# Sliding-window attention and a gated feed-forward layer: batch 0 prepared unit by unit on TensorE

## The chip, the cores and the metric

The kernel runs on one core of a Trainium2 chip. The metric is the device time of one execution in microseconds (us), given as the median of several runs. The core has a matrix engine (TensorE, PE in the profile; its weight loads have a row of their own, PEld), a vector engine (VectorE, DVE), a scalar engine (ScalarE, ACT), GpSimd (POOL) and SyncE (SP). DMA transfers are issued from a queue on SP, ACT or POOL; here POOL issues all loads that change the type from float32 to float16, and SP the output and the first loads. Matmuls read SBUF and write PSUM; DVE and ACT read both.

## What is computed

```python
# q, k, v: 8 batches x 8 heads x 576 positions x 64, float32
scores = scale * q @ k.T                        # scale = 1/8
mask = (rel >= 0) & (rel < 64)                  # rel = query position - key position
attn = softmax(where(mask, scores, -1e9))
x = (attn @ v), heads side by side              # 4608 tokens x 512
out = (relu(x @ w_gate) * (x @ w_val)) @ w_out  # 512 -> 1536 -> 512
```

## The kernel before

The 4608 tokens are cut into 24 units of 192 (three a batch, all eight heads). Two units make a tile of 384 tokens, so there are 12 tiles. A query block of 64 needs its own 64 keys and the 64 before it; a unit is three such windows.

**The attention of a unit.** `qk_load` brings k and q of a whole batch with positions on partitions; `qk_trans` (L181) turns them with 32x32 block transposes on DVE (four of 128x576 a batch). `u_st` (L236) makes the scores, keys on partitions, in 48 matmuls of 32 rows. `u_exp` takes the exponentials on ACT, `u_mask` multiplies with the band mask on DVE. `u_pv_wide` (L302) multiplies with v, of which each head has 64 columns of ones beside its values, so that values and row sums come out together. `u_copy` copies the values out of PSUM on ACT, `u_sum` (L331) turns the sums on DVE, `u_back` takes the reciprocals and turns them back, and `u_norm` (L352) writes the normalized values to `xt`, the input of the feed-forward layer. Units 0 and 1 go another way: their mask is added to the scores as a matmul with a bias (`u_bias`, L201), and their sums come from matmuls with `ones`.

**v.** A window needs 128 rows of v. `v_load` (L188) loads each block of 64 into the upper partitions of a window, and `v_low` (L194) copies it on DVE to the lower partitions of the next one. There are three buffers, one for each unit of a batch; `v_ones` sets the columns of ones.

**The feed-forward layer.** `hidden` (L389) makes, for each of 12 blocks of 128 columns, the gate and the value product (4 matmuls each of 384 or, for one unit, 192 columns), ACT applies relu, DVE multiplies the two (L407). `output` (L447) and `output_by_rows` (L474) make the product with w_out. PSUM is split between two pools: `f_ps` with four buffers of one bank (scores of unit 0, hidden and output products) and `a_ps` with two buffers of two banks (attention).

**The order.** Each engine executes its instructions in the order of the program. The order is made by `Weaver` (L16): functions are put in with a planned time, the matmuls of the feed-forward layer advance a planned clock, and whatever is due is emitted ahead of the next matmuls. `w_load` notes a planned landing time for each third of a weight matrix (L513 to L522), and `w_need` advances the clock to it. The kernel begins with a few matmuls on zeros (`heat`, L213), the loads of batch 0, and units 0 and 1; from L578 on the feed-forward layer sets the order, and units are woven in.

Of the kernel before, what the change touches and what calls it, by code (L numbers as in the profile page):

```python
# [9 lines left out]
FP32 = mybir.dt.float32  # L10
FP16 = mybir.dt.float16
ACT = mybir.ActivationFunctionType
MUL = mybir.AluOpType.mult

# [28 lines left out]
def kernel(  # L43
# [43 lines left out]
    v16s = [persist.tile([128, UB, H, 128], FP16, name=f"v16_{i}") for i in range(UB)]  # L87
# [4 lines left out]
    ident = consts.tile([128, 128], FP16)  # L92

# [21 lines left out]
    def v_ones(i, eng):  # L115
        eng.memset(v16s[i][64 if i == 0 else 0:, 0, :, 64:128], 1.0)
        for w in range(1, UB):
            eng.memset(v16s[i][:, w, :, 64:128], 1.0)  # L118

    def k_zeros():  # L120
        nc.vector.memset(kTs[1][:, :, 0:64], 0.0)

    def constants():
        nc.vector.memset(kTs[0][:, :, 0:64], 0.0)
        nc.vector.memset(v16s[0][0:64, 0], 0.0)
        nc.vector.memset(ones, 1.0)
        nc.vector.memset(ones0, 1.0)
        nc.vector.memset(ones0[0:64], 0.0)

# [40 lines left out]
    def k_first(hh):  # L170

        k32 = nat["k32", hh] = x_sb.tile([128, S // 32 * D], FP32, name="k32", bufs=2)
        nc.sync.dma_start(k32, k[0, G * hh:G * hh + G].rearrange("h (i j) d -> (h i) (j d)", i=32))

    def k_round(hh, part, parts):
        n = S // 32 * D // parts
        if part == 0:
            nat[0, "k", hh] = a_in.tile([128, S // 32 * D], FP16, name=f"k{hh}", bufs=2)
        nc.scalar.copy(nat[0, "k", hh][:, n * part:n * part + n], nat["k32", hh][:, n * part:n * part + n])  # L179
# [8 lines left out]
    def v_load(u):  # L188
        b, uu = divmod(u, UB)
        for w in range(UB):  # L190
            k0 = U * uu + 64 * w
            nc.gpsimd.dma_start(v16s[uu][64:128, w, :, 0:64], v[b, :, k0:k0 + 64].rearrange("h p d -> p h d"))  # L192

    def v_low(u):  # L194

        uu = u % UB
        if uu > 0:
            nc.vector.tensor_copy(v16s[uu][0:64, 0, :, 0:64], v16s[uu - 1][64:128, UB - 1, :, 0:64])
        nc.vector.tensor_copy(v16s[uu][0:64, 1:UB, :, 0:64], v16s[uu][64:128, 0:UB - 1, :, 0:64])

    def u_bias(u, gs=range(G)):  # L201
# [4 lines left out]
        d["biased"] = True  # L206
# [29 lines left out]
    def u_st(u, hhs=(0, 1)):  # L236
# [3 lines left out]
        if not biased:  # L240
            st_tiles(u)
# [30 lines left out]
    def u_pv(u, cs=(0, 2, 1, 3)):  # L272
        if u > 1:
            return u_pv_wide(u)
# [351 lines left out]
```

The softmax here doesn't subtract the row's maximum and nothing guards it: scores larger than these inputs give would overflow.

## Time and profile before

| | |
|---|---|
| median of 5 runs | 339.07 us (338.83 to 340.18) |
| the profiled execution: its time | 339.07 us |
| the profiled execution: its span | 337.2 us |
| PE busy | 323.4 us, 96% of the span |
| DVE busy | 260.2 us, 77% |
| ACT busy | 176.5 us, 52% |
| POOL busy | 74.0 us, 22% |
| first feed-forward matmul | 17.17 us |

The profile is that of one execution. The span runs from the first to the last instruction; the time of the execution is 1.87 us longer. A row of busy tenths has 40 slices of equal length, of 8.4 us here. In a list of groups, the numbers behind the count are the busy time in us and the mean of one in ns, then the idle time of the engine just ahead of the group and what ended it. In a timeline, a line gives start and length in us, engine, source line and operation; "[0.83 <-DVE xt L356]" means that the engine stood idle for 0.83 us and that the write of xt on line 356 ended it. The chain of waits follows the work back from the last instruction, at each step to what released it. Busy time of PE is modelled: a PE that is always busy need not be at its peak.

### The profile page before, as it was taken

How to read it: one execution, taken by the hardware profiler on the slowest of the kernel's cores; microseconds unless marked ns; L12 is line 12 of the kernel's file. 1: busy time of each engine (PE TensorE's matmuls, PEld its weight loads, DVE VectorE, ACT ScalarE, POOL GpSimd, SP SyncE). 2: the span in 40 equal slices, each digit the busy share in tenths (PEclk: the TensorE clock that was granted, in tenths of full speed). 3: DMA queues.
4: the chain of work that ended last, by engine and by line, in shares of the span. 5: the costliest groups of instructions: out<-in, count | busy, mean ns of one | idle time of the engine just before them, and what ended most of it. 6: DMA issues, size and time to landing. Idle time of an engine off the chain costs nothing.

```text
span 337.2 us, 8605 instructions
## 1 busy us (share of the span) xinstructions
PE 323.4 (96%) x3522; PEld 195.8 (58%) x3522; DVE 260.2 (77%) x493; ACT 176.5 (52%) x383; POOL 74.0 (22%) x121
## 2 busy tenths in 40 slices
PE   7689998999999999999999999999999999999995
PEld 3475485856546656655655655654655664664653
DVE  5878969988998875897888984888889874884430
ACT  4546165745637546645555565564564664653321
POOL 8724342240213221320210410150120200000000
PEclk9999999999999999999999999999999999999999
DMA  8999997395343932491242953295214502001002
GB/s 215 178 207 198 203 212 130 25 150 87 26 78 49 156 66 56 32 187 64 18 54 72 116 82 87 18 150 116 18 10 111 32 3 93 2 2 73 22 0 95
DMA packets 52887, 29.45 MB, mean 87 GB/s; under 512 B 39280, under 2 KB 44272, under 8 KB 52848
## 3 DMA queue, kind: packets, MB, share of 16 engines
q0 software_dynamic: 47088, 18.29, 47.3%
q1 hardware_dynamic: 5616, 10.55, 8.7%
q8 instruction: 27, 0.44, 0.5%
q14 instruction: 12, 0.10, 0.1%
q10 hardware_dynamic: 144, 0.07, 0.1%
HBM read 37.75 MB, written 9.44 MB: 140 GB/s over the span
## 4 chain that ended last, share of the span: by engine, by line
PE 79%; DVE 12%; DMA 5%; issue 2%; ACT 1%; DVEq 0%; ACTq 0%; POOLq 0%
PE h L419 49%; PE op L433 22%; DMA q<-in_q_dram 5%; PE pv L311 4%; PE st L249 3%; DVE qT L186 2%; DVE sT L341 2%; DVE xt L356 2%; DVE kT L186 1%; DVE g_sb L407 1%; DVE rs L350 1%; DVE p L270 1%; PE op L465 1%; ACT xv L325 1%; DVE v L118 1%
## 5 line engine op out<-in xcount | busy, mean ns | idle before, releaser
L419 PE MATMUL h<-xt,wg 128*128 128x384 f16 (+1 forms) x640 | 116.2, 310 | 2.7 <-DVE xt L356 2.7
L419 PE MATMUL h<-xt,wv 128*128 128x384 f16 (+1 forms) x640 | 116.3, 310 | 1.0 <-DVE g_sb L407 1.0
L407 DVE TENSOR_TENSOR g_sb<-r_sb,h 128x384 f16<-128x384 f32 x144 | 78.1, 549 | 48.3 <-PE h L419 46.6
L404 ACT ACTIVATE r_sb<-h 128x384 f32<-128x384 f32 x144 | 70.1, 492 | 66.6 <-PE h L419 54.8
L433 PE MATMUL op<-wo,g_sb 128*128 128x512 f16 x420 | 93.0, 379 | 0.0
L192 POOL DMA_DIRECT2D v<-in_v_dram x72 | 49.5, 697 | 180.3 <-PE pv L311 94.9
L419 PEld LDWEIGHTS <-wg 128*128 128x128 f16 x640 | 60.5, 98 | 37.6 <-DVE xt L356 2.6
L419 PEld LDWEIGHTS <-wv 128*128 128x128 f16 x640 | 58.7, 98 | 31.7 <-issue 1.3
L433 PEld LDWEIGHTS <-g_sb 128*128 128x128 f16 x420 | 40.3, 98 | 46.5
L341 DVE STREAM_TRANSPOSE sT<-pv 64x384 f32<-64x384 f32 x88 | 51.1, 580 | 9.7 <-PE pv L311 7.7
L329 ACT COPY xv<-pv 64x384 f32<-64x384 f32 x88 | 41.5, 472 | 21.3 <-DVE sT L341 8.2
L440 ACT COPY o_sb<-op 128x512 f32<-128x512 f32 x35 | 20.5, 586 | 54.6 <-PE op L433 54.6
L263 ACT ACTIVATE p<-st 128x384 f16<-128x384 f32 x92 | 39.7, 491 | 4.2 <-PE st L249 4.1
L270 DVE TENSOR_TENSOR p<-p,mask 128x384 f16<-128x384 f16 x88 | 27.5, 352 | 0.3 <-ACT p L263 0.2
L350 DVE STREAM_TRANSPOSE rs<-rT 128x768 f32<-128x768 f32 x24 | 23.5, 978 | 0.8
L356 DVE TENSOR_TENSOR xt<-xv,rs 128x768 f16<-128x768 f32 x24 | 22.7, 948 | 0.8
L311 PEld LDWEIGHTS <-v 128*128 128x128 f16 x528 | 18.6, 98 | 3.9 <-issue 0.8
L186 DVE STREAM_TRANSPOSE kT<-k 128x576 f32<-128x576 f32 (+1 forms) x18 | 19.7, 1121 | 1.3 <-ACT k L179 1.2
L311 PE MATMUL pv<-p,v 128*128 128x64 f16 x528 | 19.7, 193 | 0.8 <-DVE p L270 0.6
L186 DVE STREAM_TRANSPOSE qT<-q 128x576 f32<-128x576 f32 x16 | 19.0, 1238 | 1.1 <-DMA q<-in_q_dram 1.1
L249 PEld LDWEIGHTS <-kT 32*128 32x128 f16 x1152 | 11.0, 92 | 10.5 <-issue 10.4
L249 PE MATMUL st<-qT,kT 32*128 32x64 f16 x1152 | 13.9, 189 | 2.8 <-DVE qT L186 2.5
(47 smaller groups left out, 90.6 us busy)
## 6 DMA issues: line engine op xcount, KB each, us to landing
out_dram<-o_sb SPq DMA_DIRECT2D x35, 256.0 KB, 2.0
q<-in_q_dram POOLq DMA_DIRECT2D x16, 288.0 KB, 7.6
v<-in_v_dram POOLq DMA_DIRECT2D x72, 64.0 KB, 3.1
k<-in_k_dram POOLq DMA_DIRECT2D x14, 288.0 KB, 5.8
wg<-in_moe_w_gate_dram POOLq DMA_DIRECT2D x3, 512.0 KB, 10.0
wv<-in_moe_w_val_dram POOLq DMA_DIRECT2D x3, 512.0 KB, 12.1
wo<-in_moe_w_out_dram POOLq DMA_DIRECT2D x3, 512.0 KB, 13.8
k<-in_k_dram SPq DMA_DIRECT2D x2, 576.0 KB, 3.9
```

The costliest lines, as they stand in the source:

```text
L186: nc.vector.transpose(dst.rearrange("p (i j) -> p j i", i=32)[:, j0:j1], src[:, j0:j1])
L192: nc.gpsimd.dma_start(v16s[uu][64:128, w, :, 0:64], v[b, :, k0:k0 + 64].rearrange("h p d -> p h d"))
L249: nc.tensor.matmul(d["st"][hh][g][:, c:c + 64], kT[rows, hh, ks + 64 * w:ks + 64 * w + 128, dh], qT[rows, hh, ks + 64 * w:ks + 64 * w + 64 ...
L263: nc.scalar.activation(d["p"][g].rearrange("p h c -> p (h c)"), d["st"][0][g][:, 0:2 * U], ACT.Exp, scale=scale)
L270: nc.vector.tensor_tensor(p, p, mask[:, None, :].to_broadcast([128, 2 * UB, 64]), MUL)
L311: nc.tensor.matmul(d["pv"][c % 2][:, c // 2, e, 64 * w:64 * w + 64], v16[:, w, 128 * h - 64 * e:128 * h - 64 * e + 128], d["p"][h % G][:, ...
L329: nc.scalar.copy(d["xs"][rows, n::2], d["pv"][n][rows, :, e, 0:U])
L341: nc.vector.transpose(to[64 * e:64 * e + 64, half::2], d["pv"][half][64 - 64 * e:128 - 64 * e, :, e, 0:U])
L404: nc.scalar.activation(part(r_sb), part(h1), ACT.Relu)
L407: nc.vector.tensor_tensor(g_sb[:, f:f + w, c0:c1], part(r_sb), part(h2), MUL)
L419: nc.tensor.matmul(h[:, b * n:b * n + n], wt[:, c, (f + b) * 128:(f + b) * 128 + 128], xt[:, c, c0:c1], start=(c == 0), stop=(c == NC - 1))
L433: nc.tensor.matmul(op, g_sb[:, f, bass.ds(sub * 128, 128)], wo[:, f], start=(f == 0), stop=(f == NF - 1))
```

## The change

Units 0 to 2, the whole of batch 0, are prepared one by one. k and q of such a unit, all heads, come in one transfer each, positions on partitions (`all_load`; unit 0's in float32 by SP, rounded half on DVE and half on ACT). TensorE turns them with matmuls against a permuted identity (`turn`), 24 each, and `unit_keep` copies the result from PSUM into `kA` and `qA` with 64 rows a head. The scores are 24 matmuls of 64 rows; all three units get their mask as a bias. The row sums are made first, by matmuls with ones (`n_sums`); `n_turn` turns them, takes the reciprocals and turns back, two heads' pairs at a time; the values follow (`n_vals`), and `n_norm` multiplies them out of PSUM straight into `xt`, without a copy.

v has one buffer for a whole batch, two in all, with nine windows. Four odd windows are loaded with 128 partitions and the last half window by itself (five transfers a batch in place of nine), and `v_spread` copies their halves to the even windows, on GpSimd, for units 4 and 5 on ACT. The fixed parts of v and k (ones, zeros) are set on GpSimd.

Units 3 to 5 get k and q by units too (`unit_loads`, four transfers; `unit_trans`, four block transposes of 128x192). From batch 2 on k and q are handled as before; their early transposes are planned 1.2 us ahead of where they were. The output of tile 0 is moved behind the first half of tile 1's hidden part, and the planned times are new.

```diff
-    v16s = [persist.tile([128, UB, H, 128], FP16, name=f"v16_{i}") for i in range(UB)]
+    kA = persist.tile([128, G, 64 + S], FP16)
+    qA = persist.tile([128, G, S], FP16)
+    NG = S // 64
+    v16s = [persist.tile([128, NG, H, 128], FP16, name=f"v16_{i}") for i in range(2)]
...
+    def v_fixed(i, eng, parts=((0, NG),)):
+        for g0, g1 in parts:
+            eng.memset(v16s[i][:, g0:g1, :, 64:128].bitcast(FP32), ONE_ONE)
+        eng.memset(v16s[i][0:64, 0].bitcast(FP32), 0.0)
...
+        nc.vector.tensor_copy(turn, ident.rearrange("p (i h) -> p h i", h=H))
...
+    def unit_flip(name, u):
+        flipped[name, u] = a_ps.tile([128, 2, 512], FP32, name=f"{name}f", tag="a")
+        to = flipped[name, u].rearrange("p a b -> p (a b)")
+        for j in range(JA):
+            for hh in range(2):
+                nc.tensor.matmul(to[64 * hh:64 * hh + 64, 64 * j:64 * j + 64],
+                                 nat[name, u][:, D * j:D * j + D],
+                                 turn[:, G * hh:G * hh + G],
+                                 start=True, stop=True, skip_group_check=True)
+
+    def unit_keep(name, u, cc, copy):
+        c0 = U * u + (64 if name == "k" else 0)
+        gs_ = slice(2 * cc, 2 * cc + 2)
+        src = flipped[name, u].rearrange("p a b -> p (a b)")[:, 0:64 * JA].rearrange("p (j g i) -> p g i j", j=JA, g=G)
+        dst = (qA if name == "q" else kA)[:, gs_, c0:c0 + U].rearrange("p g (i j) -> p g i j", j=JA)
+        copy(dst, src[:, gs_])
...
+    def v_spread(u, copy=None):
+        b, uu = divmod(u, UB)
+        t = v16s[b % 2]
+        copy = copy or nc.vector.tensor_copy
+        for g0, g1 in (((0, 3),), ((4, 5),), ((6, 7),))[uu]:
+            copy(t[64:128, g0:g1:2, :, 0:64], t[0:64, g0 + 1:g1 + 1:2, :, 0:64])
+        for g0, g1 in (((2, 3),), ((4, 5),), ((6, 9),))[uu]:
+            copy(t[0:64, g0:g1:2, :, 0:64], t[64:128, g0 - 1:g1 - 1:2, :, 0:64])
...
         if u == 0:
-            d["st"] = [[one("st") for _ in range(G)]]
-            halves = [two("st") for _ in range(2)]
...
+            d["st"] = [None] * G
+            for c in (0, 2, 1, 3):
+                d["st"][c] = f_ps.tile([128, 512], FP32, name="st", tag="h")
+            d["spare"] = d["st"][3][:, 384:512]
...
+            halves = [a_ps.tile([128, 2, 512], FP32, name="st", tag="a") for _ in range(2)]
+            d["st"] = [halves[g % 2][:, g // 2] if u < UB else halves[g // 2][:, g % 2] for g in range(G)]
...
+    def n_turn(u, r):
+        d = units[u]
+        nb = 2 * U // 32
+        sN = a_n.tile([128, nb, 32], FP32, name="sN")
+        nc.vector.transpose(sN.rearrange("p b c -> p (b c)"), d["sums"][r])
+        rN = a_n.tile([128, nb, 1], FP32, name="rN")
+        nc.vector.reciprocal(rN, sN[:, :, 0:1])
+        d["rs", r] = a_n.tile([128, nb, 32], FP32, name="rsN")
+        nc.vector.transpose(d["rs", r], rN.to_broadcast([128, nb, 32]))
+
+    def n_norm(u, r):
+        d = units[u]
+        c0 = U * (u % 2)
+        nc.vector.tensor_tensor(xt_tile(u // 2)[:, r::2, c0:c0 + U],
+                                d["pv"][r].rearrange("p (s c) -> p s c", s=2),
+                                d["rs", r].rearrange("p (s b) c -> p s (b c)", s=2), MUL)
...
-        W.at(T + (3.3 if u == 2 else 1.4 if u < 6 else -2.0), lambda: v_low(u))
+        if u > 5:
+            W.at(T - 3.0, lambda: v_spread(u, nc.gpsimd.tensor_copy))
...
-        heat(12, units[0]["st"][1][3])
+        heat(9, units[0]["st"][3])
         bands()
+        for name in "kq":
+            all_load(name, 1)
+        v_load(0, ((1, 0, 128), (3, 0, 64)))
+        v_load(1, ((3, 64, 128), (5, 0, 128)))
+        for wt, t in ((G3[0], 14.4), (V3[0], 17.0), (G3[1], 19.6)):
+            w_load(*wt, t)
+        all_load("k", 2)
         constants()
...
+        all_round("k", 0, (dve, act))
+        all_round("q", 0, (dve, act))
+        unit_flip("k", 0)
+        u_bias(0)
+        unit_flip("q", 0)
+        for name in "kq":
+            unit_keep(name, 0, 0, dve)
+            unit_keep(name, 0, 1, act)
+        heat(4, units[0]["spare"], False)
+        u_st(0)
+        for c in order:
+            u_exp(0, c)
+        for name in "kq":
+            unit_flip(name, 1)
+            for cc in range(2):
+                unit_keep(name, 1, cc, act)
+        v_spread(0, pool)
+        v_spread(1, pool)
+        all_load("q", 2)
+        v_load(2)
+        for wt, t in ((V3[1], 25.6), (G3[2], 28.2), (V3[2], 30.8)):
+            w_load(*wt, t)
+        v_fixed(1, nc.gpsimd)
+        unit_loads(3)
+        v_spread(2, pool)
+        v_load(3)
+        for n in range(3):
+            w_load(*O3[n], 38.2 + 2.6 * n)
...
+        for r in range(2):
+            n_sums(0, r)
+            n_turn(0, r)
+        heat(3, flipped["k", 1][:, 1, 256:512])
+        for r in range(2):
+            n_vals(0, r)
+            n_norm(0, r)
+        u_bias(1)
+        u_st(1)
+        for c in order:
+            u_exp(1, c)
+        for r in range(2):
+            n_sums(1, r)
+            n_turn(1, r)
...
+        finish_unit(1, 15.75, 0.01)
+        W.at(23.4, lambda: [unit_flip(name, 2) for name in "kq"] and None)
+        W.at(23.5, lambda: [unit_keep(name, 2, cc, act) for name in "kq" for cc in range(2)] and None)
+        W.at(24.2, lambda: u_bias(2))
+        W.at(24.8, lambda: u_st(2))
...
+        for u, t in ((3, 39.5), (4, 49.5), (5, 57.5)):
+            plan_trans(u, t - 3.2)
+            if u > 3:
+                W.at(t + 0.5, lambda u=u: v_spread(u, act))
+            plan_unit(u, t)
-        T = 67.0
-        early, late = (-7.4, -6.0, -4.6, -3.2), (-20.3, -18.9, -17.5, -16.1)
+        T = 69.3
+        early, late = (-8.6, -7.2, -5.8, -4.4), (-20.3, -18.9, -17.5, -16.1)
...
-        output_by_rows(0)
         ready(3)
         hidden(1, 0, U)
+        output_by_rows(0)
         output(1, (0,))
```

## The prediction

> **What bounds the kernel now.** I read the page's busy shares and slices first, the chain of waits second, then the timelines of TensorE (PE) and GpSimd (POOL), and the groups by shape for prices.
>
> ```profile
> PE 323.4 (96%) x3522; PEld 195.8 (58%) x3522; DVE 260.2 (77%) x493; ACT 176.5 (52%) x383; POOL 74.0 (22%) x121
> PE   7689998999999999999999999999999999999995
> DMA  8999997395343932491242953295214502001002
> ```
>
> PE is full from the third slice on, so the end moves only with the start of the feed-forward matmuls, with PE work added or removed after it, and with the gaps that remain. The transfers are nearly full for seven slices of 8.4 us, to about 59 us.
>
> ```profile
> 1.31 6.02 DMA q<-in_q_dram
> 7.36 1.26 DVE qT L186
> ...
> 16.16 0.96 DVE xt L356
> ...
> 119.37 7.77 PE op L433 x36
> ...
> 171.98 7.77 PE op L433 x36
> ...
> 197.93 7.77 PE op L433 x36
> ```
>
> The chain (start, length) runs through the load of q, the block transposes on VectorE (DVE), unit 0's softmax and the write of xt before PE may start. Later it is PE alone: from one tile's output to the next it is 197.93-171.98 = 25.95 us, but 52.61 us for the two tiles 119.37 to 171.98. So 0.71 us is lost there; the same occurs from 197.93 to 250.54.
>
> ```profile
> 17.17 1.48 PE L419 MATMUL h<-xt,wg 128*128 128x192 f16 x16 [0.83 <-DVE xt L356]
> 35.62 7.93 PE L433 MATMUL op<-wo,g_sb 128*128 128x512 f16 x36
> 74.10 0.81 PE L419 MATMUL h<-xt,wg 128*128 128x384 f16 x4
> ```
>
> These three marks are my yardstick: the first feed-forward matmul at 17.17, the hidden part of tile 0 done at 35.62, tile 2 begun at 74.10.
>
> ```profile
> 17.89 0.76 POOL L151 DMA_DIRECT2D wo<-in_moe_w_out_dram  x1 [2.35 <-DMA wv<-in_moe_w_val_dram]
> 23.17 0.74 POOL L151 DMA_DIRECT2D wo<-in_moe_w_out_dram  x1 [2.02 <-DMA wv<-in_moe_w_val_dram]
> L407 DVE TENSOR_TENSOR g_sb<-r_sb,h 128x384 f16<-128x384 f32 x144 | 78.1, 549 | 48.3 <-PE h L419 46.6 <-ACT r_sb L404 0.3
> L341 DVE STREAM_TRANSPOSE sT<-pv 64x384 f32<-64x384 f32 x88 | 51.1, 580 | 9.7 <-PE pv L311 7.7
> L350 DVE STREAM_TRANSPOSE rs<-rT 128x768 f32<-128x768 f32 x24 | 23.5, 978 | 0.8
> L199 DVE COPY v<-v 64x1024 f16<-64x1024 f16 x24 | 10.4, 433 | 0.2
> L98 POOL MEMSET ident<- 128x128 f16 x1 | 0.2, 244 | 0.0
> L97 POOL MEMSET mask<- 128x64 f16 x1 | 0.2, 190 | 0.0
> ```
>
> The first two lines date the landing of the first two thirds of w_val: 17.9 and 23.2 us (POOL starts when they land). The rest are prices.
>
> [...] no GpSimd copy is in this trace, only memsets (190 ns for 64, 244 ns for 128 elements: 0.84 ns an element, 0.14 us fixed). [...] the L199 copy, 0.42 us as a rule, took 0.74 us at 13.96 us while POOL issued transfers. [...] 40 half-width matmuls (L289, L296) went by in 1.09 us from 11.55, 27 ns each.
>
> **The start.** The first k and q loads shrink to one unit each (384 KB in place of 576 KB twice, both on SP). The k loads move at about 415 GB/s once running (SP's two landed by about 4.2 and 5.6 us), so I put unit 0's k at 3.7 and q at 4.6. Nine heating matmuls hold PE to about 5.0 (the twelfth ended at 5.6). 24 turning matmuls at 27 ns with an end delay of 0.2, four bias matmuls of 384 columns (0.65), 24 more: q is in PSUM at 6.7. Two copies of 384 elements each (ACT 0.48 after the 64x384 row, DVE 0.55 after L407) run on both engines: 7.2. Scores 0.4, four exps at 0.41 (1.65 for four at 14.12): 9.3. PE queues unit 1's turning (0.8) ahead of the sums; it waits for POOL's loads, no later than 8.5. Sums 0 are there at 9.0; a turn on DVE is 0.58 + reciprocal 0.25 (between 0.2 and the 0.30 of 24 values) + 0.55, so two end at 11.9.
>
> The values wait for more. POOL first makes the bands (1.56), then issues ka, qa (0.6 each), four v pieces (0.7 to 1.0), three weight loads (0.8), ka, in all about 7.8 us: it reaches its first v copy at 10.3. The copies are 1024 and 512 elements: 1.6 us at the memset slope, [...] I take 2.1, so v is whole at 12.4. Values 0.5, unit 1's bias 0.65, half its scores 0.4, its four exps 1.65, the last sums 0.25: the feed-forward starts at 15.85 (15.3 to 16.4), **1.3 us ahead** of 17.17. Unit 1's sums stand in front of it on PE, so its exps are on the path.
>
> **To the end of tile 0's hidden part.** 16+16 matmuls at 0.083 with unit 1's values (0.4) between: 18.95. xt of unit 1 waits for DVE (two turns to 17.85, two multiplies of 0.55): 19.1. 32 more: 21.75. 16 of 384 columns (0.1625): 24.35. Then unit 2 is turned between these matmuls: flips 0.8 to 25.15; but the score tiles take the two PSUM buffers that the flips hold, and all four copies out are on ACT (4 x 0.48, 24.95 to 26.87). PE idles 1.45 us around bias and scores (1.05): 27.65. That the weights land late (V at 23.2 before, and three loads are now ahead of it) hides part; I take none. Then 48 matmuls 7.8, sums 0.35, values 0.4. DVE now has two turns (2.8) and two multiplies (1.1) among four gates of 0.51: the gates release the four h banks at 32.8 and 34.3 where PE would want them at 32.8 and 33.5; with the switching this costs 0.95. End: 37.15, **1.5 us later** than 35.62. So unit 2 now costs PE 2.65 us in place of 1.2, and brings two waits; that is more than the start gave.
>
> **What is moved.** Tile 0's 36 output matmuls go behind tile 1's first hidden half, with their three evictions on ACT (0.59 each) and three writes on SP: no PE work changes, and SP has nothing else to do, so I cost this at nothing; it covers the later landing of w_out, whose three loads POOL now issues after unit 3's k, q and v. If they landed after 45 us instead of the 36 of before, PE would wait for them. POOL's queue also gets the fixed parts of v (about 2 us a buffer at the memset slope) and the zeros of k; behind them stand only loads that are needed 10 us later.
>
> **To tile 2.** PE work is the same: 192 matmuls at 0.083, 72 at 0.216, three times scores 0.48 and values 0.70 and 0.22 of switching: 35.7. Before, 38.5 went by: 2.8 of gaps. Now the DVE no longer copies v (0.29+0.43 a unit; 3.9 us of memsets go to POOL, hidden there), but four 128x192 transposes a unit (0.45, as 288 took 0.70) come close ahead of their scores. After unit 4's values DVE has two sums (1.2), three transposes (1.35), two sums, one transpose: 4.2 us, where PE has 3.3 us to do. Waits: 0.25 and 0.25 at unit 4, 1.1 at unit 5's scores, 0.9 at its gates and values, the last because two v copies on ACT (1.5) and DVE's queue delay the masks: 2.5. So the stretch is 38.25, tile 2 starts at 75.4, **1.3 us late**.
>
> **The tiles after.** They gain at most the 0.71 twice and 1.0 in tile 2 (18.2 us from its kind of start to its outputs, 101.19 to 119.37, against 19.2): 2.4. k and q transposes of two batches move 1.2 us forward and DVE is 0.7 us a unit lighter: I take 0.9. Against it stand 18 units' v copies, 2.1 us each, on POOL, which may hold a mask (352 ns) or a normalization (948 ns) of DVE back; 0 if they never meet, 18 x 0.3 = 5 if each shifts PE; I take 0.7, since POOL runs far ahead and the copies follow the values of six units earlier. The removed xs copies and masks of units 0 to 2 are in the sums above.
>
> Sum: +1.3 - 0.9 + 0.7 = +1.1 on a span of 337.2; the profiled execution itself took 339.07 (1.87 around the span), which is also the median: **340.2**.
>
> **Rivals.** (1) GpSimd is quick and DVE's relief is real: copies at the memset slope (-0.5), the tile losses won back for the most part (-2.0 in place of -0.9), no sharing (0): +1.3-0.5-2.0 = -1.2, 337.9; with the waits at unit 5 also gone, 336.8. I take 337.4, on the other side. For it: DVE sheds 15.0 us of v copies and 3.9 of memsets. Against: PE shows hardly a gap for it to fill. It decides from tile losses under 0.4 us and copies under 1.6. (2) GpSimd is slow or blocked: at 2.5 ns an element the first copies take 4.1, the start is back at 17.8, and the 18 later copies hold DVE more: +1.1+2.0 = 342.2. The start's gain is gone altogether at copies of 3.4 us. (3) The weights bind: with w_val's first third after 18.5 or its second after 28, PE waits 1 us more: 341.3. For it: full transfers; against: 1.6 MB instead of 2.4 MB of k and q are read first.
>
> **Numbers.** Forecast 340.2, own range 338.9 to 341.5, chance 0.48; rival 1 0.28; rival 2 0.16; rival 3 0.08. A difference under 0.3% (1.0 us) is about what a measurement can't tell from none. Of the forecast's 0.48, 0.25 lies within it (to 340.1) and 0.23 above; of rival 1, 0.25 is faster and 0.03 within; of rivals 2 and 3, 0.02 within. Faster 0.25, same 0.30, slower 0.45. The range, 337.0 to 342.6, leaves out a tenth at each end.
>
> **What would show it.** First feed-forward matmul near 15.9, tile 0's hidden part done near 37, tile 2 near 75.4; an idle PE of over 1 us before unit 2's bias; waits of PE for DVE transposes at unit 5; POOL's first v copy of 1024 elements at 1.0 to 1.7 us. A start before 14.5, or tile 2 before 74, would prove the forecast wrong.

## The result and the profile after

| | before | changed |
|---|---|---|
| median | 339.36 us (338.62 to 341.53, 48 runs) | 342.98 us (339.18 to 344.47, 27 runs) |
| ratio, changed to before | | 1.0086, 95% interval 1.0068 to 1.0104 |
| the profiled execution: time, span | 339.07, 337.2 | 339.54, 337.8 |

The kernel became slower by 0.9%. On the 339.07 of the prediction the ratio makes 342.0; the forecast was 340.2, its range 337.0 to 342.6. The median says little by itself, because the executions of the changed kernel fall into two groups: of the 28 whose clock is recorded 8 have a mean granted TensorE clock of 1.00 and a median of 339.5, 20 have 0.985 to 0.99 and a median of 343.2. The kernel before has a milder form of it: of 128 executions measured beside the experiments 48 had at least 0.998 (median 338.95), 77 about 0.995 (339.39), three less. So two questions are to be answered: why the changed kernel is 0.55 us slower at full clock, and why most of its executions lose 3.7 us more.

The execution profiled first is one at full clock. From its page, busy time and the rows of slices:

```profile
PE 326.2 (97%) x3584; PEld 196.2 (58%) x3584; DVE 238.0 (70%) x449; ACT 177.1 (52%) x379; POOL 106.4 (31%) x150
PE   7697999999999999999999999999999999999996
PEclk9999999999999999999999999999999999999999
DMA  9999999899759531449329722405002002001002
```

DVE lost 22 us of work, POOL gained 32, and PE got 2.8 us more. The fourth slice of PE (25 to 34 us) is down at 7. The timeline of PE shows the marks of the prediction and the waits between them (start, length, operation, idle time ahead and what ended it). Here and below single lines of a view are picked out, in their order:

```profile
12.38 0.44 PE L369 MATMUL pv<-p,v 128*64 128x64 f16 x16 [0.42 <-POOL v L267]
15.86 0.36 PE L354 MATMUL sums<-p,ones 128*64 128x192 f16 x4 [0.68 <-DVE sN L380]
16.14 1.49 PE L506 MATMUL h<-xt,wg 128*128 128x192 f16 x16
24.73 0.57 PE L224 MATMUL kf<-turn,ka 128*64 128x64 f16 x24
26.25 0.48 PE L275 MATMUL st<-bias,ident 128*128 128x384 f16 x2 [0.57 <-ACT kA L235]
27.02 0.48 PE L275 MATMUL st<-bias,ident 128*128 128x384 f16 x2 [0.28 <-ACT qA L235]
33.92 0.38 PE L369 MATMUL pv<-p,v 128*64 128x64 f16 x12 [1.41 <-DVE xt L389]
38.80 0.82 PE L506 MATMUL h<-xt,wg 128*128 128x192 f16 x8
76.26 0.81 PE L506 MATMUL h<-xt,wg 128*128 128x384 f16 x4
```

The feed-forward begins at 16.14, 1.03 us ahead of before; tile 0's hidden part is done at 38.80, 3.2 us late; tile 2 begins at 76.26, 2.16 us late. From there to the end 261.5 us go by in place of 263.1. In the chain of waits (start, length) these are some of the tiles' outputs:

```profile
94.86 7.77 PE op L520 x36
120.81 7.77 PE op L520 x36
173.22 7.77 PE op L520 x36
199.16 7.77 PE op L520 x36
```

One tile takes 25.95 us (94.86 to 120.81), as before. Two tiles take 52.41 (120.81 to 173.22), where they took 52.61. The first output matmuls of tile 1 began 2.03 us later than before (70.95 for 68.92), the first of the last tile 1.03 us later (326.67 for 325.64): 1.0 us is won back between, 0.58 of it up to tile 2's output. Another 0.4 us is won back at the very end (5.95 us in place of 6.38 from the start of the last row block's output to the end of the span); the cause of that stays open.

### The profile page after: what moved, and what is told of

The parts are those of the page before. It is cut to its first block, busy times and chain, and to the rows that moved or that the text cites. A ratio compares the mean times of both kernels' runs of the same rounds, so it can differ in the third digit from the quotient of the medians.

```text
span 337.8 us, 8658 instructions
## 1 busy us (share of the span) xinstructions
PE 326.2 (97%) x3584; PEld 196.2 (58%) x3584; DVE 238.0 (70%) x449; ACT 177.1 (52%) x379; POOL 106.4 (31%) x150
## 4 chain that ended last, share of the span: by engine, by line
PE 84%; DVE 8%; ACT 2%; DMA 2%; issue 2%; POOL 1%; POOLq 0%; DVEq 0%; ACTq 0%
PE h L506 54%; PE op L520 21%; PE pv L405 4%; PE st L318 3%; DVE sT L427 2%; DMA v<-in_v_dram 2%; DVE kT L250 1%; DVE g_sb L494 1%; DVE xt L442 1%; PE op L552 1%; ACT p L328 1%; DVE rs L436 1%; DVE sN L380 1%; ACT o_sb L527 0%; DVE p L338 0%
## 5 line engine op out<-in xcount | busy, mean ns | idle before, releaser
L256 POOL DMA_DIRECT2D v<-in_v_dram x41 | 34.4, 844 | 93.5 <-PE pv L405 93.4
L427 DVE STREAM_TRANSPOSE sT<-pv 64x384 f32<-64x384 f32 x84 | 48.8, 581 | 9.8 <-PE pv L405 8.0
L419 ACT COPY xv<-pv 64x384 f32<-64x384 f32 x84 | 39.6, 472 | 21.0 <-DVE sT L427 9.0
L328 ACT ACTIVATE p<-st 128x384 f16<-128x384 f32 x96 | 41.7, 490 | 4.5 <-PE st L305 2.8
L265 POOL COPY v<-v 64x512 f16<-64x512 f16 (+1 forms) x22 | 17.7, 803 | 16.2 <-DMA v<-in_v_dram 15.4
L436 DVE STREAM_TRANSPOSE rs<-rT 128x768 f32<-128x768 f32 x21 | 20.5, 978 | 0.7
L442 DVE TENSOR_TENSOR xt<-xv,rs 128x768 f16<-128x768 f32 x21 | 20.0, 952 | 0.4
L405 PE MATMUL pv<-p,v 128*128 128x64 f16 x504 | 18.7, 193 | 0.5 <-DVE p L338 0.3
L267 POOL COPY v<-v 64x512 f16<-64x512 f16 (+1 forms) x22 | 17.9, 815 | 1.1
L250 DVE STREAM_TRANSPOSE kT<-k 128x576 f32<-128x576 f32 x12 | 14.9, 1241 | 0.2
L250 DVE STREAM_TRANSPOSE qT<-q 128x576 f32<-128x576 f32 x12 | 14.3, 1230 | 0.0
```

Source lines behind the costliest of these rows:

```text
L250: nc.vector.transpose(dst.rearrange("p (i j) -> p j i", i=32)[:, j0:j1], src[:, j0:j1])
L256: nc.gpsimd.dma_start(v16s[b % 2][lo:hi, g, :, 0:64], v[b, :, 64 * g - 64 + lo:64 * g - 64 + hi].rearrange("h p d -> p h d"))
L328: nc.scalar.activation(d["p"][g].rearrange("p h c -> p (h c)"), d["st"][g][:, 0:2 * U], ACT.Exp, scale=scale)
L405: nc.tensor.matmul(d["pv"][c % 2][:, c // 2, e, 64 * w:64 * w + 64], v16[:, w, 128 * h - 64 * e:128 * h - 64 * e + 128], p_of(u, h)[:, 64 ...
L419: nc.scalar.copy(d["xs"][rows, n::2], d["pv"][n][rows, :, e, 0:U])
L427: nc.vector.transpose(to[64 * e:64 * e + 64, half::2], d["pv"][half][64 - 64 * e:128 - 64 * e, :, e, 0:U])
```

## The experiments

Two theories stood at the start. *Clock*: in most executions the start is so sparse on PE that the granted clock falls. *Order*: the change's own waits cost the time at full clock. Rivals were late transfers, and VectorE as the new bound.

### The kernel once more, and three single edits

**e1_again**: no edit.

> The changed kernel unchanged, for a second profile. Of its executions so far some ended near 339.5 us with a mean granted TensorE clock of 1.00, more of them near 343 with 0.985 to 0.99. Clock theory: if this one falls near 343, its profile shows one stretch of a few microseconds in which the granted clock is about half and matmuls take twice their time, 3 to 4 us are lost there and none elsewhere; the stretch lies in the first 40 us, where TensorE has its gaps. Rival: the loss is spread over the whole span, in waits for GpSimd's copies or for transfers, and the lower mean clock only follows from it. Near 339.5 it tells neither.

It took 342.76 us, span 341.1, mean clock 0.99. The windows of its trace (span of the window, its length, then busy time and instructions of PE, PEld, DVE, ACT and POOL, the granted clock, and two figures of the transfers that aren't used here):

```profile
10.20:13.60 3.40, 1.44 (x39) 0.95 (x33) 2.66 (x6) 1.38 (x4) 2.02 (x4) 1.00 1.62 180
13.60:17.00 3.40, 1.98 (x46) 1.11 (x39) 1.65 (x4) 1.64 (x4) 3.34 (x6) 0.68 1.24 205
17.00:20.40 3.40, 3.40 (x32) 2.69 (x34) 2.03 (x5) 0.68 (x2) 3.35 (x4) 0.50 1.28 202
```

The same windows in the execution at full clock:

```profile
10.20:13.60 3.40, 2.34 (x41) 1.36 (x42) 3.26 (x8) 1.39 (x4) 2.80 (x4) 1.00 1.38 180
13.60:17.00 3.40, 1.94 (x43) 1.56 (x43) 1.84 (x5) 1.64 (x4) 3.40 (x6) 1.00 1.24 205
17.00:20.40 3.40, 3.40 (x61) 3.20 (x59) 2.98 (x7) 1.12 (x3) 2.90 (x3) 1.00 1.30 205
```

The clock is 0.50 from 14.8 to 21.6 us (by windows of 0.2 us) and full elsewhere. Both executions keep PE busy for the whole of 17.0 to 20.4, but one does 32 matmuls there and the other 61: busy time doesn't show a halved clock, the count and the clock column do. Ahead of the fall PE was busy for only 1.44 of 3.40 us. A sparse window doesn't bring a fall each time, though. The kernel before, in its execution at full clock, has a sparser one:

```profile
13.60:17.00 3.40, 1.32 (x32) 1.08 (x33) 3.23 (x7) 1.86 (x5) 1.54 (x3) 1.00 1.24 205
```

6.8 us at half clock are 3.4 us lost of 341, which is the mean clock of 0.99. By the same reckoning 0.995 is about 3.4 us at half clock and 0.985 about 10.2. These are estimates; the traces of h1 below (3.4 us, 0.994) and f3 (10.2 us, 0.984) agree with them. No trace was taken of an execution of the changed kernel at 0.985.

Why PE was sparser than in the other execution is told by POOL's timeline, here that of e1_again:

```profile
11.57 1.03 POOL L265 COPY v<-v 64x1024 f16<-64x1024 f16 x1 [1.26 <-DMA v<-in_v_dram]
12.66 0.61 POOL L267 COPY v<-v 64x512 f16<-64x512 f16 x1
```

and that of the execution at full clock:

```profile
10.62 1.03 POOL L265 COPY v<-v 64x1024 f16<-64x1024 f16 x1 [1.14 <-DMA v<-in_v_dram]
11.71 0.61 POOL L267 COPY v<-v 64x512 f16<-64x512 f16 x1
```

v landed 0.95 us later, and PE stood 1.12 us for the first copy (first line), where it had stood 0.17 (second line, full clock):

```profile
12.65 0.25 PE L369 MATMUL pv<-p,v 128*64 128x64 f16 x4 [1.12 <-POOL v L265]
11.71 0.25 PE L369 MATMUL pv<-p,v 128*64 128x64 f16 x4 [0.17 <-POOL v L265]
```

The marks split the loss: the feed-forward begins at 17.43 (1.29 late: 0.95 for v, the rest sums at half clock), unit 2's turning at 27.89 (3.16 late, so 1.87 more), and tile 2 at 79.41 (3.15 late): nothing is lost from unit 2 on. So in this execution neither the tiles nor GpSimd's later copies have a part in the 3.2 us.

**e2_order**: nothing but the order of emission, so that no PSUM tile is read between two writes of its halves.

```diff
         for r in range(2):
             n_sums(1, r)
+        for r in range(2):
             n_turn(1, r)
-        finish_unit(2, 28.3, 0.8)
+        finish_unit(2, 28.3, 0.01)
```

> Both halves of unit 1's sums are emitted ahead of both turns, and both halves of unit 2's values ahead of both multiplies, so that no half waits for a VectorE read of the other half of the same PSUM tile. Shared-tile theory: the 0.68 us ahead of unit 1's second sums and the 1.41 us ahead of unit 2's second values go, tile 0's hidden part ends 1.4 to 2.1 us earlier (36.6 to 37.3 in place of 38.7), span of executions with full clock 336.0 to 336.6 in place of 337.8. Rival, VectorE binds: the same time is waited for its gates and turns, span 337.5 to 338. Clock: if the lower clock comes from the sparse first 16 us, about 7 of 10 executions still lie 3 to 4 us higher; if it comes from the gaps between 25 and 34 us, clearly fewer.

Median 340.14, ratio to before 1.0019 (0.9999 to 1.0038). Executions at 0.998 or more: 8 of 20, median 338.35, 1.15 us under those of the changed kernel. From the timeline of PE:

```profile
15.78 1.14 PE L354 MATMUL sums<-p,ones 128*64 128x192 f16 x8 [0.79 <-ACT p L328]
34.42 0.57 PE L369 MATMUL pv<-p,v 128*64 128x64 f16 x24
```

Both halves now go by in one piece. From unit 2's turning to the first matmul of tile 1 it takes 12.45 us (27.77 to 40.22) in place of 14.07: 1.6 us, within the range of the shared-tile theory; VectorE was not the bound there. Of that and of the 0.68 us ahead of unit 1's second sums 1.15 us reach the end. The clock still fell to 0.99 or less in 10 of 20 executions, in the profiled one at 15.2 us. So the fall doesn't need the gap of 34 us. Whether that gap has a part can't be told: 10 of 20 against 20 of 28 is a difference that chance can make.

**e3_keep**: unit 2's k is copied out by DVE.

```diff
-[unit_keep(name, 2, cc, act) for name in "kq" for cc in range(2)]
+[unit_keep(name, 2, cc, act if name == "q" else dve) for name in "kq" for cc in range(2)]
```

> Unit 2's k is copied out of PSUM by VectorE, which is idle there for 5.96 us, its q by ScalarE as before. Queue theory: the waits of 0.57 and 0.28 us ahead of unit 2's bias shrink to about 0.6 in all at most, the scores come 0.4 to 0.6 us sooner, span with full clock 337.2 to 337.5 in place of 337.8. Rival: what comes after is bound by unit 2's exponentials and turns on VectorE, so that the gain is given back, span 337.7 to 338. Clock: as in the run with the order changed, a smaller gap at 25 to 28 us tells whether that gap has part in the lower clock.

Median 343.1 of four runs, clock 0.99 or less in three. PE waits once for 0.74 us in place of 0.57 and 0.28, and the stretch from turning to tile 1 is 13.80 us for 14.07. That is a gain of 0.27, below what was expected, and too small to see in the times.

**e4_before_early**: the kernel before with `early` set to (-8.6, -7.2, -5.8, -4.4).

> The kernel before, with nothing but the tuple changed that sets when VectorE transposes a batch's k and q: 1.2 us sooner. From tile 2 on the changed kernel needs 1.56 us less than the one before. Tuple theory: the waits of 1.1 us for qT after 80 us go by this alone, and the kernel before gets 1.0 to 1.5 us faster (span 335.7 to 336.2 in place of 337.2). Rival: it is the lighter VectorE (copies of v on GpSimd) that wins them back, and this kernel stays within 0.3 us of the one before or gets slower, since the transposes now stand in front of other work.

Median 338.48, ratio 0.9984 (0.9973 to 0.9995). The waits for qT are gone, and the two late tiles take 26.45 and 26.46 us in place of 26.67 and 26.66; the way to tile 2's output remains at 24.33. So in the trace the tuple (the planned times in `early`) is worth 0.4 us, not 1.0 to 1.5: of the 1.1 us for qT in the waits PE lost only part. The span is 0.7 us shorter, but 0.3 of that is there already when tile 0's hidden part is done (35.31 for 35.62), ahead of all that the edit moves.

### Is it the sparse start?

**f1_heat**: the gaps are filled with multiplications by zeros. `spare` are 128 unused columns of the bank that takes the second half of unit 0's values.

```diff
-        heat(3, flipped["k", 1][:, 1, 256:512])
+        heat(24, spare, False)
...
         for w in (1, 0, 2):
+            if (u, r, w) == (0, 0, 2):
+                heat(6, d["spare"], False)
...
         u_st(1)
+        heat(12, spare, False)
```

> The changed kernel, with the gaps of TensorE between 10.4 and 15 us filled by multiplications with zeros into spare columns of a PSUM bank: 24 of 128 columns after unit 0's sums in place of 3 of 256, 6 more ahead of the last part of its values, 12 after unit 1's scores. Clock theory (the sparse stretch after unit 0's sums, longer when v lands a microsecond late, halves the granted clock for some 7 us): mean clock 0.998 to 1.00 in nearly all executions, times 339 to 341 with a median near 339.9, no group near 343. Rival, late transfers: when v lands late, all that follows is 3 to 4 us late whatever TensorE does meanwhile, and the two groups stay. Rival, another stretch: the clock still falls, since the thinnest stretch is elsewhere (5 to 8 us or 25 to 28 us).

Median 342.02 of five runs, clock 0.995 to 1.00. The clock is kept in the profiled execution, although v was 0.65 us late:

```profile
10.20:13.60 3.40, 3.06 (x60) 2.48 (x60) 2.76 (x7) 1.38 (x4) 2.21 (x3) 1.00 1.44 187
13.60:17.00 3.40, 2.32 (x44) 1.47 (x42) 1.00 (x3) 1.75 (x4) 3.34 (x6) 1.00 1.24 205
```

and from the first feed-forward matmul to unit 2's turning it took 8.59 us, as at full clock (10.46 in e1_again). But the time came out 2 us over what was expected, and two of the five runs still lie at 342.87 and 343.45, with 0.995. The filling stood in the way, with 0.84 us ahead of unit 1's sums, and with an idle stretch inside unit 1's scores:

```profile
14.15 0.35 PE L305 MATMUL st<-qA,kA 64*128 64x64 f16 x12
15.28 0.35 PE L305 MATMUL st<-qA,kA 64*128 64x64 f16 x12 [0.78 <-issue]
15.56 0.84 PE L282 MATMUL pv<-zero 128*128 128x128 f16 x12
```

"issue" means that the profile shows nothing it waited for. In f2_heat_order_keep it ends at 15.26, almost at the same time, although the scores began 0.3 us sooner there. It occurs only in these two kernels, with 39 matmuls more than the changed one ahead of the feed-forward; its cause stays open.

**f2_heat_order_keep**: f1_heat with e2_order's and e3_keep's edits.

> The filled gaps together with the two edits of order (both halves of sums and of values emitted ahead of what reads the first half; unit 2's k copied out by VectorE). If the three losses are separate, they add: full clock in nearly all executions, 1.6 us off by the order, 0.3 to 0.5 by the copy: median 337.6 to 338.4, ahead of the kernel before by 1 us or more. Rival, overlap: once one wait is gone, VectorE's chain of turns and gates holds the rest, median 338.5 to 339.3.

Median 339.96, ratio 1.0016 (1.0003 to 1.0030), clock 0.998 or more in all 12 executions. The stretch from turning to tile 1 is 12.20 us, the sum of both gains. The median misses both ranges. Tile 2 begins at 77.18, since new waits appear behind:

```profile
PE h L510 <- DVE xt L446: 1.3, 2, 0.7
PE h L510 <- ACT o_sb L531: 0.9, 1, 0.9
PE pv L409 <- DVE p L338: 0.7, 1, 0.7
```

(Waits of PE from 46 us on: total, times, longest.) ACT's waits in the same stretch name the cause of the second:

```profile
ACT o_sb L531 <- DMA out_dram<-o_sb: 2.6, 1, 2.6
```

The eviction of tile 1's first row block, the fourth into three buffers, waits for the write of a row block of tile 0; PE then lacks a PSUM bank for 0.9 us. The waits for xt have another cause, GpSimd's copies, which are the subject of the last section of the experiments: two multiplies that write xt took 1.73 and 1.36 us in place of 0.94. g1_order_wide_heat below begins tile 1 at the same time (38.11 for 38.14) and has neither of these waits; there tile 2 begins 1.8 us sooner.

**f3_before_no_heat**: the other way round, the kernel before without its second and third group of heating.

```diff
-        W.at(5.4, lambda: heat(11, units[0]["spare"], False))
-        W.at(9.5, lambda: heat(11, units[0]["spare"], False))
```

> The kernel before without two of its three groups of heating multiplications (11 after unit 0's bias, 11 between the two halves of its scores); nothing else is changed, and their results are not used. Clock theory: TensorE is then busy for less than half of the time between 6 and 12 us, the granted clock falls to half for about 7 us in most executions, and the time rises by 2 to 4 us to 341.5 to 343. Rival: the lower clock of the changed kernel comes from its order of work, the heating does nothing here, and the time stays at 339.4.

```profile
6.80:10.20 3.40, 0.90 (x31) 0.63 (x28) 2.20 (x4) 0.54 (x4) 2.64 (x4) 0.98 1.89 164
10.20:13.60 3.40, 2.12 (x56) 1.51 (x58) 2.00 (x5) 1.51 (x7) 3.29 (x5) 0.50 1.73 171
13.60:17.00 3.40, 2.66 (x78) 1.73 (x74) 2.73 (x8) 2.48 (x8) 2.13 (x4) 0.50 1.24 208
17.00:20.40 3.40, 3.40 (x43) 3.00 (x39) 3.23 (x8) 1.80 (x6) 0.76 (x1) 0.52 1.24 205
```

The heating holds the clock up: without it, it is halved from 10.0 to 20.2 us, and 15 of 20 executions have 0.99 or less, where of the 128 with heating three have. But the time rises only to 339.98, ratio 1.0018 (1.0009 to 1.0027), not by the 2 to 4 us expected. Part of the kernel before's own executions have a short fall, so the ratio is too low a price; between the two profiled executions the span grows by 1.1 us (338.3 for 337.2). Ten microseconds at half clock thus cost 1.1 us here and seven cost about 2.2 in the changed kernel. Here most of them lie where PE waits for DVE anyway (feed-forward at 18.17 for 17.17), there more than half lie over dense feed-forward matmuls.

**f4_v_on_dve**: `v_spread(u)` in place of `v_spread(u, nc.gpsimd.tensor_copy)` for units 6 and later.

> The changed kernel with the copies of v of units 6 and later back on VectorE (1024 and 512 elements by 64 partitions, about 0.43 and 0.26 us), nothing else. Relief theory: the 0.58 us that tile 2 lost less, and perhaps part of the later 0.2 us twice, come from the lighter VectorE, and come back: from tile 2's start to the end 0.5 to 1 us longer than the 261.5 of the changed kernel. Rival: VectorE has room there, and the gain is that of the earlier transposes: within 0.2 us of 261.5. Sharing: if copies on GpSimd held VectorE's masks and multiplies up, their mean would fall from 357 and 952 ns.

Median 349.31, ratio 1.0267 (1.0225 to 1.0309). A miss: 266.3 us from tile 2 to the end (81.79 to 348.1), not 262 to 262.5. Only these 4.8 us over the changed kernel's 261.5 price the copies: ahead of tile 2 the clock fell twice, from about 14.1 to 20.9 us and, behind the wait of 2.00 us below, from about 68.7 to 72.1.

```profile
67.56 0.82 PE L506 MATMUL h<-xt,wv 128*128 128x192 f16 x8 [2.00 <-ACT o_sb L527]
122.41 0.81 PE L506 MATMUL h<-xt,wg 128*128 128x384 f16 x4 [0.39 <-DVE g_sb L494]
```

A tile takes 26.45 us in place of 25.95. At 121.03 and 121.48 two copies run in front of three gates that PE waits for. The kernel before had its copies on DVE too, 1 us later in the plan, and its tiles took 25.95; so this prices a bad place as much as the relief, and h1 below is the cleaner measure. Masks and multiplies took 351 and 946 ns here, 357 and 952 with the copies on GpSimd. The means hide what single instructions show: the longest mask took 0.36 us here and 0.77 there, the longest multiply 0.96 and 1.07 (see the last section of the experiments).

### Two ways to keep the clock

**g1_order_wide_heat**: e2_order's edit, and wide filling in the buffer that was heated before: `heat(9, ...)` in place of `heat(3, ...)`, 4 more ahead of the last part of the values, nothing behind.

> The changed kernel with the edit of order alone (both halves of unit 1's sums and unit 2's values ahead of what reads the first half) and the gap after unit 0's sums filled by few, wide multiplications with zeros: 9 of 256 columns in place of 3, and 4 more ahead of the last part of the values; nothing after unit 1's scores, where the earlier filling met an idle stretch of 0.8 to 1.1 us that no event of the profile explains. Clock theory, with that stretch put down to the 78 instructions added: no idle stretch in unit 1's scores, mean clock 0.998 to 1.00 in most executions, first feed-forward matmul at 16 to 17, median 337.8 to 338.6. Rival: filling costs as much as it saves, or the clock falls all the same: median 339.5 to 340.5 as with the order alone (340.1).

Median 339.21 (338.72 to 339.41), ratio 0.9998 (0.9985 to 1.0012), 0.998 or more in all 12 executions, no idle stretch in the scores. PE's busy time in the windows 10.2 to 13.6 and 13.6 to 17.0 is 2.69 and 2.48 us. The group near 343 is gone with ten more matmuls; the median is between the two theories. The feed-forward begins at 16.55, as expected (16 to 17); why the time is still 0.6 us over the expected range stays open.

**g2_v_first**: nothing filled, but v sooner.

```diff
+        v_load(0, ((1, 0, 128), (3, 0, 64)))
         for name in "kq":
             all_load(name, 1)
-        v_load(0, ((1, 0, 128), (3, 0, 64)))
...
-        for name in "kq":
-            unit_flip(name, 1)
-            for cc in range(2):
-                unit_keep(name, 1, cc, act)
...
         for r in range(2):
             n_sums(0, r)
             n_turn(0, r)
+        for name in "kq":
+            unit_flip(name, 1)
+            for cc in range(2):
+                unit_keep(name, 1, cc, act)
```

> The changed kernel with unit 0's two v pieces issued by GpSimd ahead of unit 1's k and q, and unit 1's turning moved behind unit 0's sums; nothing is filled. Landing theory (the lower clock begins where TensorE waits for GpSimd's first copies of v, which wait for v): the first copy starts near 9.5 to 10 in place of 10.6 to 11.9, TensorE has no wait of over 0.5 us for it, and executions with a mean clock under 0.992 become the exception; median near 339.5. Rival: unit 1's k and q now land late, TensorE waits for them instead, the stretch before the feed-forward stays as sparse, and most executions stay near 343.

```profile
9.78 1.03 POOL L265 COPY v<-v 64x1024 f16<-64x1024 f16 x1
10.87 0.61 POOL L267 COPY v<-v 64x512 f16<-64x512 f16 x1
```

The copies have no wait ahead of them, all 20 executions have 0.994 or more, the median is 340.24 (339.76 to 341.24), ratio 1.0033 (1.0021 to 1.0044). It is 0.7 us over the changed kernel's executions at full clock (q of unit 0 lands later, feed-forward at 16.84), and 2.7 under its median. So the landing theory holds as to the clock, not as to the time (339.5). The edit does two things, though: v comes sooner, and unit 1's 48 turning matmuls now stand in the gap behind unit 0's sums, where PE is busy for 2.62 us of 10.2 to 13.6 in place of 1.44. Which of the two keeps the clock isn't told apart. f1 and g1 show that filling the gap is enough, although v landed late in them (first copy at 11.27 and 11.33).

### What is worth keeping

**h1_before_pool_copies**: the kernel before with the tuple and, for units 6 and later, `v_low` on GpSimd at T - 3.0.

> The kernel before with two parts of the change alone: the earlier tuple for k and q, and the copies of v of units 6 and later on GpSimd, planned 1 us sooner; the whole start, the order of tile 0 and the masks stay as before. Parts theory: the start of before (tile 2 begun near 73.8 us) and the tiles of the changed kernel (261.5 us from there) add up: span 335.3 to 335.8, median 337.2 to 337.7, ahead of both kernels. Rival: the copies block GpSimd's queue, on which the loads of k, q and v wait, or tile 2's gain belongs to the changed kernel's order; the tiles stay at 262.7, median near 338.5.

Median 338.71, ratio 0.9984 (0.9972 to 0.9996). The tiles are as expected, 261.7 us from 74.94 to the end. From tile 1's first output to the last tile's first it takes 255.87 us; before 256.72, e4 256.30, the changed kernel 255.72: the tuple is worth 0.42, GpSimd's copies with their earlier plan 0.43. But tile 2 begins 1.1 us later than expected, and in the time the copies bring nothing: the ratio is that of e4, which has the tuple alone. The clock fell for about 3.4 us from 15.2 (the windows 13.6 to 17.0 and 17.0 to 20.4 show 0.73 and 0.77), but that isn't it: tile 0's hidden part is done at 35.41, where e4 has 35.31. PE waited twice 0.5 us for masks ahead of unit 5's values, where it had waited once for 0.28:

```profile
67.19 1.10 POOL L200 COPY v<-v 64x1024 f16<-64x1024 f16 x1
L271 DVE TENSOR_TENSOR p<-p,mask x4: 345/350/1191, 66.8 to 68.9; 128x384 f16<-128x384 f16 x4
68.56 0.26 PE L312 MATMUL pv<-p,v 128*128 128x64 f16 x3 [0.48 <-DVE p L271]
```

The second line gives the shortest, median and longest of the four masks in ns. The one of 1191 ns ended at 68.51 and so began at 67.32, while GpSimd's copy ran until 68.29. In the four kernels whose later copies are on VectorE (before, e4, f3, f4) no such mask took more than 0.36 us and no multiply into xt more than 0.96. In each kernel that has them on GpSimd single ones took longer, up to 1.19 and 1.73. So the copies hold VectorE up now and then, and at least 0.67 of the 1.1 us is theirs.

**h2_v_first_order_keep**: g2_v_first with e2_order's and e3_keep's edits.

> The changed kernel with v's two pieces ahead of unit 1's k and q (which kept the clock full, 340.2), both halves of sums and values ahead of what reads the first half (1.6 us), and unit 2's k copied out by VectorE (0.25 us); nothing is filled. Sum theory: the three are separate: 340.2 - 1.6 - 0.25 = 338.4, mean clock 0.998 to 1.00, tile 2 begun near 75.1. Rival, transfers: what comes sooner meets the writes of tile 0's rows and the loads of v near 60 us, where TensorE then waits 0.5 to 1 us for ScalarE's evictions: median 338.9 to 339.4. Rival, clock: without the waits in other places the sparse stretch falls into another window and a group near 342 comes back.

Median 338.43 (337.83 to 340.33, 22 runs), ratio to before 0.9974 (0.9963 to 0.9984), the lowest of all, though its interval overlaps those of e4 and h1. The three gains add up as expected. The feed-forward begins at 15.96, and its waits of PE from 30 us on are four:

```profile
PE pv L405 <- DVE p L338: 0.8, 1, 0.8
PE h L506 <- DVE xt L442: 0.6, 1, 0.6
PE st L318 <- DVE sT L427: 0.3, 1, 0.3
PE st L318 <- DVE qT L243: 0.2, 1, 0.2
```

The two longest come from GpSimd's copies as well. For the second of them:

```profile
73.43 1.04 POOL L267 COPY v<-v 64x1024 f16<-64x1024 f16 x1
73.74 1.54 DVE L442 TENSOR_TENSOR xt<-xv,rs 128x768 f16<-128x768 f32 x1
75.34 0.81 PE L506 MATMUL h<-xt,wg 128*128 128x384 f16 x4 [0.55 <-DVE xt L442]
```

The multiply overlaps the copy for 0.73 us and takes 0.60 longer than its usual 0.94. Ahead of the first wait, a mask begun at 66.68 took 0.78 us beside a copy begun at 66.64. In g1, whose order is the same there, the multiply ran from 74.37 to 75.31 and the copy began at 75.22: it took 0.94, and tile 2 didn't wait. So a few tenths of a microsecond in the plan decide on it. A kernel with h2's order and the copies moved out of the way of masks and multiplies was not run.

## Why the prediction was right or wrong

The direction was right, and at full clock half of the forecast size came (0.55 us slower where 1.1 was forecast). The range held the ratio's 342.0, but by luck: the forecast's own range ended at 341.5, and what reached beyond it was rival 2, whose cause isn't there. What makes up most of the loss isn't in the prediction.

1. **What failed: the heating's removal was put at nothing.** "Nine heating matmuls hold PE to about 5.0" counts the PE time of the first group alone; that the groups of 12, 11 and 11 became 9, 4 and 3 has no price. e1, f1, f3 and g1 show what they were for: in e1, without them and with v late, PE was busy for 1.44 us of 3.40, and the clock was 0.50 for the 6.8 us from 14.8 on, which cost 1.9 us in the feed-forward and some 0.3 ahead of it, with the 0.95 of v itself 3.2 us in that trace; between the medians of the two groups, with 20 of 28 executions in the one near 343, it is 3.7. The clock row of the page before was full, so nothing there warned but the heating itself.
2. **The start.** 15.85 was forecast, 16.14 came (17.43 where the clock fell). k and q landed at 5.0 and 6.4, not 3.7 and 4.6; the two copies out of PSUM ran one after the other (0.35 us of ACT waiting for DVE's half of the same tile), not side by side. The sum for q in PSUM was wrong as well: its terms make 7.15, not 6.7, and 7.4 came; that does no harm to the forecast, since v's way was the longer one. GpSimd's copies made the late start good in part: 1.03 and 0.61 us, 1.64 in place of the 2.1 that was the author's estimate; the slope of the memsets had given 1.6. What was taken as the uncertain term was the safe one; how long v takes to land varied by a microsecond.
3. **Unit 2.** PE idle around the bias: 0.85 us in place of 1.45; but turning, bias and scores took 2.3 us of PE in place of 1.85, so that this part came out 0.14 better. Sums, values and switching: 1.7 us of PE in place of 0.75. The wait put at 0.95 for gates was 1.41, and of another kind: e2_order shows that it was the first half's multiply, which held the second half's values because both halves share a PSUM tile, and that without it nothing takes its place. Together with the start's 0.3 this is the 1.65 us by which tile 0's hidden part came later than forecast.
4. **The moved output.** It cost nothing, as forecast, but the risk lay elsewhere than in landing weights. In f2 and f4 ACT waits for the write of an earlier row block, and PE for 0.9 and 2.0 us. g1 and h2 reach this place as early as f2 or earlier (tile 1 begun at 38.11 and 37.27, for 38.14) and don't have the wait, so it isn't the earlier start alone; what makes the writes land late was not found.
5. **To tile 2.** 37.5 us in place of 38.25. Forecast were waits of 2.5 us, 1.1 came (0.29, 0.20, 0.29, 0.34 in the timeline).
6. **The tiles.** Forecast: 0.9 won, and 0.7 lost to copies that hold VectorE up, which was the author's estimate. Measured: 1.0 won up to the last tile's output, of which 0.42 belongs to the tuple and about 0.43 to GpSimd's copies (h1, e4), and next to nothing lost to such copies (PE's wait for a mask ahead of unit 5's values is 0.34 us in place of 0.28). But that was luck in the timing: the loss is real in other kernels, where PE waits for a held mask or multiply (0.48 and 0.47 us in h1, 0.77 and 0.55 in h2, 0.67, 0.74 and 0.55 in f2). What the two engines share there was not shown.

The forecast was near at full clock because its misses cancel: 1.65 us too early up to tile 0's hidden part, 0.8 too late from there to tile 2, 1.4 too late in the tiles and the tail. Of its rivals, the first (GpSimd quick, losses in the tiles won back) had the tiles right and the way there wrong; the second had the number by accident, for the first copies were quicker than taken, and the later ones held VectorE without a loss; the third fell, as no wait of PE ends with a weight's landing.

## What to carry to other kernels

Before you shorten or remove multiplications that compute nothing, ask what they hold up (without its second and third group the kernel before ran at a granted clock of 0.50 for 10.2 us in f3): look at the granted clock by windows of a few microseconds, in several executions, not at the busy shares. A median over executions with different clocks mixes two kernels (339.5 and 343.2 us here); read them apart, and look for the landing or wait that decides which one an execution becomes. Of two halves that shared a PSUM tile the second waited until VectorE had read the first (0.68 and 1.41 us, gone with the order of e2_order): write both ahead of the first read. When work moves to GpSimd, look at the longest single VectorE instruction beside it, not at the mean: 357 ns for 351 hid masks of 0.77 us.

## What the hardware showed

- The granted clock was 0.50 for 6.8 us in e1_again, e2_order and e3_keep and for 10.2 us in f3_before_no_heat, by windows of 0.2 us; in h1_before_pool_copies 0.73 and 0.77 in two windows of 3.4 us make about 3.4 us at half clock, an estimate. PE was not idle throughout ahead of the fall in e1_again: in the 3.4 us from 10.2 it was busy for 1.44. A limit can't be read from such figures, since 1.32 us in the 3.4 from 13.6 did not bring a fall in the kernel before.
- What the halved clock cost differed with what lay under it: 1.1 us between the profiled executions for 10.2 us mostly of waits and small matmuls (f3), about 2.2 us for 6.8 us that reach into dense ones (e1).
- The same transfer, v's first piece, had landed when GpSimd's first copy began, at 10.62 us in the changed kernel's execution at full clock and at 11.57, 11.58 and 11.87 in e1, e2 and e3, which have the same start; so a spread of a microsecond is to be reckoned with there.
- A GpSimd copy of 64 partitions in float16 took 1.03 us for 1024 elements and 0.61 for 512 at the start of the changed kernel (0.42 and 0.29 on DVE in f4); from two sizes that is 0.82 ns an element and 0.19 us, an estimate. Later copies of the changed kernel had means of 1.04 to 1.06 and 0.66 to 0.71 us, since some were held (up to 1.21 and 1.44).
- Where a GpSimd copy and a VectorE instruction with both inputs in SBUF overlapped, one or both took longer: a mask took 1.19 us in place of 0.35 (h1), a multiply 1.54 in place of 0.94 (h2). It went the other way too: in the changed kernel a copy of 512 elements, begun at 65.78 inside a multiply begun at 65.62, took 1.27 us in place of 0.61, while the multiply took its 0.94. The multiplies into g_sb, which read one input from PSUM, took at most 0.556 us with the copies on GpSimd and 0.555 without (f4).
